# Attention's product with v in plain 32-bit floats, each head in its own half of TensorE's columns

## The chip, the cores and the metric

One core of one Trainium2 chip runs the whole kernel. The metric is the device time of one execution in microseconds (us), and lower is better. The engines are TensorE (PE, with its weight loads as PEld), VectorE (DVE), ScalarE (ACT), GpSimd (POOL) and SyncE (SP, which here only issues transfers).

## The reference

Attention with a threshold feeds a layer of 8 experts with two of them per token, and that feeds a dense layer. Only attention is touched:

```python
scores = q @ k.T / 8                          # 4 batches, 8 heads, 576 positions, 64 features
thresh = scores.max(-1) - tau
attn   = exp(where(scores >= thresh, scores, -1e9) - scores.max(-1))
out    = (attn / (attn.sum(-1) + 1e-9)) @ v
# x = out, heads side by side: (2304, 512)
# experts: gate and noise logits of x, top 2 of 8, relu(x @ w1) @ w2
# dense: elu(x @ w_in) @ w_out
```

## The kernel before

*Work units.* The 32 heads are handled as 16 pairs P, with s = 0 and 1 for the two heads of a pair. The 576 positions are four blocks of 128 (NB = 4) and a tail of 64. A pair has nine units u: unit 0 holds the tail rows of both heads, units 1 to 8 are one block of rows of one head (`ORDER`). Each unit goes through the same steps, which single letters name in the order lists:

- S `scores` (line 236): products of q and k into a double bank of PSUM
- R `rowmax` (261) on DVE, H `thresh` (263) on DVE (its ScalarE branch is never taken, since `HA` is always false), E `expo` (270) on ACT
- M `mask` (275) on DVE: exponentials below the threshold become 0, and their sum is taken. For unit 0 POOL then copies the last 64 columns once more (line 294)
- T `trans` (302): four transposes on PE, so that keys lie on partitions
- A, L, C `evac_trans` (328): PSUM to SBUF, as two tiles of rounded floats (`F32R`), high (`pth`) and low (`ptl`). High is a copy on ACT (line 324 or 320). Low is what is left of the sum: for seven units a PE product with the negative identity `negi` subtracts the high half in PSUM, and ACT copies the rest (325, 326); for units 0 and 2 DVE subtracts (321).

Per pair come the steps t, a, d `tails` (345): transposes of the tail keys, and their high and low halves; p, q `pv` (366): the product with v, for each head and each of two chunks of query columns (320 and 256 wide); W `weigh`: one over the sums; f, g `fin` (395): products that turn the result back to rows and multiply it with the gate weights `wx`, a copy on ACT, and the scaling on POOL.

*The product with v.* v is split by POOL into high and low halves (`split_v`, 226), side by side in 128 columns. One `pv` call makes ten products (four blocks and the tail, each with the high and the low half of the exponentials) into all 128 partitions: 64 of v's high half and 64 of its low half. The two are added in `fin`, whose weights hold the identity twice. `fin`'s operands (`ot`, `wx`) are plain 32-bit floats.

*Order.* PE, ACT and DVE run in an order written by hand: the strings `FIRST` (pair 0 alone), `CYCLE` (each further pair; the number behind the dot says how many pairs back the step belongs to) and `REST` (what is left). G and F advance the expert gate of a finished batch, W and X other small steps. POOL and SP are ordered by the program and its dependences. `load(P + 2)` fetches q, k and v two pairs ahead; `split_q` and `split_k` on POOL and copies on SP's queue prepare the next pair's scores.

After attention come the experts (from line 759) and the dense layer (from line 1029), which the change leaves as they are.

Of the kernel before, what the change touches and what calls it, by code (L numbers as in the profile page):

```python
# [25 lines left out]
def fused_kernel(ctx, tc, q, k, v, tau, w_gate, noise, wm, wf, out):  # L26
# [56 lines left out]
    negi = consts.tile([128, 128], F32R, name="negi")  # L83
    dve.tensor_scalar(negi, iot, 0.0, -1.0, op0=OP.is_equal, op1=OP.mult)
# [29 lines left out]
    for nm, sh, dt, n in (("qr", [128, S], F32, 2), ("kr", [128, S], F32, 2), ("vr", [128, NU, D], F32, 2),  # L114
# [31 lines left out]
    wx = apool.tile([128, HP, D + 4 * E], F32, name="wx", bufs=1)  # L146
# [4 lines left out]
    def load(P):  # L151

        t = []
        for nm, src in (("qr", q), ("kr", k), ("vr", v))[0 if P else 2:]:
            x = apool.tile([128, S], F32, name=nm)
# [4 lines left out]
        RAW[P] = t  # L160

# [64 lines left out]
    def split_v(P):  # L226
        vr = RAW[P][-1].rearrange("p (i d) -> p i d", d=D)
        vs = apool.tile([128, 2 * NB, 2, D], F32R, name="vs")
        vt = vts[P % 2]
        for hi, lo, x in [(vs[:, :, 0], vs[:, :, 1], vr[:, :2 * NB])] + \  # L230
                [(vt[r, s, 0], vt[r, s, 1], vr[r, 2 * NB]) for s, r in ((0, slice(0, 64)), (1, slice(64, 128)))]:
            rounded(hi, x, pool)
            pool.tensor_tensor(lo, x, f32(hi), op=OP.subtract)
        VS[P] = (vs, vt)

# [39 lines left out]
    def mask(g):  # L275
# [38 lines left out]
    def halves(P, s, c):  # L314
        if (P, s, c) not in PTH:
            PTH[P, s, c] = tuple(apool.tile([128, NB, CW[c]], F32R, name=f"pt{x}{s}{c}", bufs=1) for x in "hl")
        return PTH[P, s, c]

    def evac(o_hi, o_lo, ps):
        return (lambda: act.activation(o_hi, ps, AF.Copy),  # L320
                lambda: dve.tensor_tensor(o_lo, ps, f32(o_hi), op=OP.subtract))  # L321

    def evac_pe(o_hi, o_lo, ps):
        return (lambda: act.activation(o_hi, ps, AF.Copy),  # L324
                lambda: pe.matmul(ps, negi, o_hi, start=False, stop=True, skip_group_check=True),  # L325
                lambda: act.activation(o_lo, ps, AF.Copy))  # L326

    def evac_trans(g):

        P, u = divmod(g, NU)  # L330
        ps = PS_.pop(g)
        if u:
            i, s = ORDER[u]
            h, l = halves(P, s, i // 2)
            c = (i % 2) * 128 + (TAIL if s and i < 2 else 0)
            r = (evac_pe if VP(P, u) and P not in EVEN else evac)(h[:, :, c:c + 128], l[:, :, c:c + 128], ps)
            return [r[:1], r[1:-1], r[-1:]]
        r = []
        for s in range(2):
            h, l = halves(P, s, 0)  # L340
            c = 0 if s else 256
            r.append(evac(h[:, :, c:c + 64], l[:, :, c:c + 64], ps[:, :, s * 64:s * 64 + 64]))
        return [x[0] for x in r], [], [x[1] for x in r]

    def tails(P, half):
        ps = mi(512)
        for n in range(2):
            turn(ps[:, n * 128:n * 128 + 128], P_[P, 2 * half + n][1][:, MAIN:MAIN + 128], F32R)
        if not half:
            turn(ps[:, 256:384], PTB[1][:, MAIN:], F32R)  # L350
        cols = ((0, 0, 256),) if half else ((64, 0, 320), (0, 320, 64))

        def high():
            PTT[P, half] = tuple(apool.tile([128, 384 - 128 * half], F32R, name=f"ptt{x}{half}", bufs=1) for x in "hl")
            for o, i, n in cols:
                act.activation(PTT[P, half][0][:, o:o + n], ps[:, i:i + n], AF.Copy)

        def low():
            for o, i, n in cols:
                h, l = (x[:, o:o + n] for x in PTT[P, half])  # L360
                dve.tensor_tensor(l, ps[:, i:i + n], f32(h), op=OP.subtract)
        return high, low

    OC = ((256, 0), (S, S + 320))

    def pv(P, s, ch):
        vs, vt = VS[P]
# [3 lines left out]
        ps = mi(512)
        steps = [(kb, x) for kb in range(NB + 1) for x in range(2)]
        for m, (kb, x) in enumerate(steps):
            if kb < NB:
                lhs = vs[:, s * NB + kb]
                rhs = PTH[P, s, ch][x][:, kb]
            else:
                lhs = vt[:, s]
                o = 0 if s or ch else TAIL
                rhs = PTT[P, ch][x][:, o:o + n]  # L380
# [899 lines left out]
```

## Time and profile before

| what | value |
|---|---|
| median of 3 runs | 1244.54 us (1244.17 to 1246.15) |
| the profiled execution itself | 1239.1 us |
| its span, first to last instruction | 1237.3 us |
| mean granted TensorE clock | 0.985 |

The profile is one execution of its own. Rows of a trace give the start and the duration of an instruction; TensorE's instructions overlap, so the distance between two starts tells what one costs the engine, and the duration tells how long it is in flight. A plain 32-bit product appears as two records, each with a weight load.

### The profile page before, as it was taken

The numbers are of one execution on the slowest core, as the hardware profiler recorded it, in microseconds if no ns is written. First come the engines' busy times: TensorE is split into PE (matmuls) and PEld (weight loads), VectorE is DVE, ScalarE is ACT, GpSimd is POOL, SyncE is SP. The second block draws the span as 40 slices with busy tenths as digits, with TensorE's granted clock in tenths as the row PEclk, the third lists the DMA queues.
The fourth block names the chain that finished last, engine by engine and source line by source line (L and its number), as shares of the span: only waits on it lengthen the run. The fifth ranks groups of instructions, "written<-read, shape, count | busy, mean of one in ns | idle before, by whom it ended". The sixth has DMA issues, their size and how long they took to land.

```text
span 1237.3 us, 20812 instructions
## 1 busy us (share of the span) xinstructions
PE 1187.9 (96%) x7675; PEld 1088.4 (88%) x7675; DVE 751.7 (61%) x1663; ACT 650.7 (53%) x1324; POOL 320.5 (26%) x502
## 2 busy tenths in 40 slices
PE   4999999989889999999999999899999999999997
PEld 3899999989779998998998898788999889999996
DVE  6899999979764886656665557355343333333332
ACT  3899999879633443333333332256554554444443
POOL 8546657786650111000010001311011010000000
PEclk8999999999989999999999999899999999999999
DMA  7577674552466785465555544443123021010000
GB/s 214 170 209 205 191 213 124 157 174 80 171 235 241 233 269 180 163 194 166 185 178 154 177 138 171 153 165 126 43 63 92 17 70 41 11 51 19 1 17 20
DMA packets 64044, 169.50 MB, mean 137 GB/s; under 512 B 9408, under 2 KB 9536, under 8 KB 58304
## 3 DMA queue, kind: packets, MB, share of 16 engines
q1 hardware_dynamic: 52768, 138.45, 36.2%
q0 software_dynamic: 5760, 18.88, 4.5%
q10 hardware_dynamic: 5408, 10.78, 2.4%
q8 instruction: 62, 1.02, 0.4%
q14 instruction: 46, 0.38, 0.1%
HBM read 97.72 MB, written 43.52 MB: 114 GB/s over the span
## 4 chain that ended last, share of the span: by engine, by line
PE 73%; issue 10%; DVE 6%; DMA 6%; POOL 3%; ACT 2%; SPq 0%; POOLq 0%; ACTq 0%; DVEq 0%
PE y L877 17%; PE h L861 16%; PE o L1070 11%; PE h L1051 11%; PE bank L252 6%; PE bank L381 5%; PE bank L164 3%; PE bank L408 2%; PE bank L325 2%; DMA yg<-ys_d,yslot 2%; DMA w<-in_moe_dram 1%; PE h L164 1%; DVE P L289 1%; DVE nmax L261 1%; POOL yg L774 1%
## 5 line engine op out<-in xcount | busy, mean ns | idle before, releaser
L1059 DVE SCALAR_TENSOR_TENSOR g<-fr,h 128x256 f32<-128x256 f32 x144 | 60.3, 420 | 173.1 <-ACT fr L1058 172.8
L864 ACT ACTIVATE hh<-h 128x320 fp32r<-128x320 f32 (+2 forms) x128 | 55.5, 434 | 159.1 <-PE h L861 149.6
L845 POOL TENSOR_TENSOR c<-c,c 128x512 int32<-128x512 int32 x32 | 41.4, 1293 | 372.1 <-DVE c L844 372.1
L261 DVE TENSOR_REDUCE nmax<-bank 128x1 f32<-128x576 f32 x144 | 107.6, 753 | 19.4 <-PE bank L252 17.7
L1057 ACT ACTIVATE fr<-h 128x256 f32<-128x256 f32 x144 | 54.9, 382 | 118.1 <-PE h L1051 118.0
L273 ACT ACTIVATE e<-bank,nmax 128x576 f32<-128x576 f32 x144 | 106.6, 748 | 15.9 <-DVE nmax L261 14.0
L252 PE MATMUL bank<-kT,qT 128*128 128x288 f32 x320 | 98.5, 323 | 16.3 <-DVE kT L191 8.2
L774 POOL DMA_INDIRECT yg<-ys_d,yslot x36 | 39.0, 1083 | 269.8 <-PE h L164 170.2
L865 DVE SCALAR_TENSOR_TENSOR hl<-h,hh 128x320 fp32r<-128x320 f32 (+2 forms) x128 | 62.3, 487 | 67.5 <-ACT hh L864 67.0
L289 DVE SCALAR_TENSOR_TENSOR P<-bank,thr,e 128x576 f32<-128x576 f32 x128 | 100.0, 807 | 3.8 <-ACT e L273 1.9
L1061 DVE TENSOR_TENSOR gl<-g,gh 128x256 fp32r<-128x256 f32 x144 | 61.0, 425 | 67.5 <-ACT gh L1060 66.6
L252 PE MATMUL bank<-kT,qL 128*128 128x288 f32 x320 | 92.7, 305 | 0.8 <-DVE qL L199 0.8
L1060 ACT ACTIVATE gh<-g 128x256 fp32r<-128x256 f32 x144 | 59.8, 416 | 63.4 <-DVE g L1059 63.4
L252 PEld LDWEIGHTS bank<-kT,qT 128*128 128x128 f32 x320 | 62.6, 196 | 23.5 <-DVE P L289 10.7
L326 ACT ACTIVATE ptl<-bank 128x512 fp32r<-128x512 f32 x107 | 65.0, 607 | 17.0 <-PE bank L325 15.7
L381 PE MATMUL bank<-pth,vs 128*128 128x320 f32 (+1 forms) x256 | 73.3, 309 | 0.0
L381 PE MATMUL bank<-ptl,vs 128*128 128x320 f32 (+1 forms) x256 | 69.8, 295 | 0.0
L324 ACT ACTIVATE pth<-bank 128x512 fp32r<-128x512 f32 x107 | 62.9, 596 | 8.4 <-PE bank L164 7.4
L164 PE MATMUL bank<-ident,P_r 128*128 128x128 f32 x576 | 63.8, 243 | 2.3 <-DVE ptl L321 1.6
L252 PEld LDWEIGHTS bank<-kT,qL 128*128 128x128 f32 x320 | 63.1, 197 | 2.3 <-DVE qL L199 1.0
L164 PEld LDWEIGHTS bank<-ident,P_r 128*128 128x128 f32 x576 | 61.1, 142 | 3.5 <-DVE ptl L321 1.8
L1058 ACT ACTIVATE fr<-fr 128x256 f32<-128x256 f32 x144 | 59.9, 417 | 4.1
(373 smaller groups left out, 3929.3 us busy)
## 6 DMA issues: line engine op xcount, KB each, us to landing
w<-in_moe_dram SPq DMA_DIRECT2D x36, 1024.0 KB, 6.3
cr<-in_ffn_dram SPq DMA_DIRECT2D x32, 512.0 KB, 4.5
xs_d<-t ACTq DMA_DIRECT2D x8, 1280.0 KB, 5.4
ys_d<-y SPq DMA_DIRECT2D x40, 256.0 KB, 2.3
xr<-xs_d SPq DMA_DIRECT2D x38, 256.0 KB, 3.5
qT<-qh SPq DMA_DIRECT2D x60, 144.0 KB, 3.4
wf_d<-c SPq DMA_DIRECT2D x32, 256.0 KB, 4.5
w<-wf_d SPq DMA_DIRECT2D x8, 1024.0 KB, 6.2
```

The source lines that it names most:

```text
L164: pe.matmul(o.bitcast(dt), x.bitcast(dt), ident.bitcast(dt), is_transpose=True, **{"start": True, "stop": True, **kw})
L252: pe.matmul(ps[:, hv, :S // 2], x[:, qc:qc + 128], kx[:, kc:kc + S // 2], start=(m == 0), stop=(m == n - 1))
L261: dve.tensor_reduce(ST[g][0], view(g), axis=AX.XY, op=OP.max, negate=True)
L273: act.activation(e, view(g), AF.Exp, bias=ST[g][0])
L289: dve.scalar_tensor_tensor(o.rearrange("p (a c) -> p a c", a=2), view(g), ST[g][1], E_.pop(g), op0=OP.is_ge, op1=OP.mult, accum_out=SU[P][ ...
L324: return (lambda: act.activation(o_hi, ps, AF.Copy), lambda: pe.matmul(ps, negi, o_hi, start=False, stop=True, skip_group_check=True), lam ...
L326: lambda: act.activation(o_lo, ps, AF.Copy))
L381: pe.matmul(ps[:, :n], lhs.rearrange("p a d -> p (a d)"), rhs, start=(m == 0), stop=(m == len(steps) - 1))
L861: pe.matmul(ps[:, :step], w[:, c, f * 128:(f + 1) * 128], x[:, c, o:o + step], start=(m == 0), stop=(m == 3 * NC1 - 1))
L877: pe.matmul(Y[t], h[:, t * 128:(t + 1) * 128], w[:, f], start=(first and m == 0), stop=(last and m == 2))
L1051: pe.matmul(ps, w[:, c, f * 128:(f + 1) * 128], x[:, c], start=(m == 0), stop=(m == 3 * NC1 - 1))
L1070: pe.matmul(O[i], h[:, i * 128:(i + 1) * 128], w[:, f], start=(un == f == m == 0), stop=(un == NU2 - 1 and f == UF - 1 and m == 2))
```

## The change

The exponentials and v are no longer split. `evac_trans` copies each transposed unit once, by ACT, into a plain 32-bit tile; `negi`, the low halves and `split_v` are gone. `pv(P, ch, part)` handles both heads of a chunk: head s writes partitions 64 s to 64 s + 63 of one bank, with 64 columns of v as weights, and products of the two heads alternate. The ten products of a chunk are issued in two parts, a (four) and b (six). The tail rows of v sit in four zeroed tiles `vt`, filled by two more loads per pair; v itself gets four buffers. The tail keys of both heads share one tile, with one more transpose, and the zeros behind unit 0 are set once in place of POOL's copy. One ACT copy empties both heads of a chunk. `fin` takes 128 query columns of both heads at once (160 output columns), and the tails in two halves. The three order lists are rewritten, with `SECOND` for the second pair.

```diff
-    negi = consts.tile([128, 128], F32R, name="negi")
-    dve.tensor_scalar(negi, iot, 0.0, -1.0, op0=OP.is_equal, op1=OP.mult)
...
-    wx = apool.tile([128, HP, D + 4 * E], F32, name="wx", bufs=1)
+    wx = apool.tile([128, HP, 2, D + 2 * E], F32, name="wx", bufs=1)
...
+        vt = vts[P % 4]
+        VS[P] = t[-1].rearrange("p (i d) -> p i d", d=D), vt
+        for s in range(2):
+            r = slice(s * 64, s * 64 + 64)
+            st = sp.dma_start(vt[r, s], v[P][r, 2 * NB * D:])
...
-    def split_v(P):
...
-        if HA(*divmod(g, NU)):
-            act.activation(thr, nmax, AF.Identity, scale=-1.0, bias=tneg)
-        else:
-            dve.tensor_scalar(thr, nmax, -1.0, tneg, op0=OP.mult, op1=OP.add)
+        dve.tensor_scalar(thr, nmax, -1.0, tneg, op0=OP.mult, op1=OP.add)
...
-        if u == 0:
-            pool.tensor_scalar(PTB[0][:, S:], PTB[0][:, MAIN:S], 1.0, 1.0, op0=OP.mult, op1=OP.mult)
...
+            act.activation(turned_p(P, s, i // 2)[:, :, c:c + 128], ps, AF.Copy)
+        else:
+            for s in range(2):
+                act.activation(turned_p(P, s, 0)[:, :, 256:], ps[:, :, s * 64:s * 64 + 64], AF.Copy)
...
-            turn(ps[:, 256:384], PTB[1][:, MAIN:], F32R)
+            for n, c in enumerate((MAIN, MAIN - 64)):
+                turn(ps[:, 256 + n * 128:384 + n * 128], PTB[1][:, c:c + 128], F32R)
...
+        if part == "a":
+            PV_[P, ch] = mi(512)
+        ps = PV_[P, ch][:, :n]
+        for kb in (range(2) if part == "a" else range(2, NB + 1)):
+            for s in range(2):
+                if kb < NB:
+                    lhs, rhs = vr[:, s * NB + kb], PTH[P, s, ch][:, kb]
+                else:
+                    lhs, rhs = vt[:, s], PTT[P, ch]
+                pe.matmul(ps[s * 64:s * 64 + 64], lhs, rhs, start=(kb == 0), stop=(kb == NB))
+        o = OC[ch]
+        return lambda: act.activation(OT[P][:, o:o + n], ps, AF.Copy)
...
+        for i in range(2):
+            c = OC[half] + i * 128
+            pe.matmul(ps[:, 2 * i * NX:2 * (i + 1) * NX], OT[P][:, c:c + 128],
+                      wx[:, j].rearrange("p a b -> p (a b)"), start=True, stop=True)
+        if not half:
+            for s in range(2):
+                pe.matmul(ps[s * 64:s * 64 + 64, n:n + NX], OT[P][:, MAIN:S], wx[:, j, s], start=True, stop=True)
...
+    pool.memset(PTB[0][:, S:], 0.0)
+    dve.memset(wx, 0.0)
...
+    CYCLE = """
+        E7.1 E8.1 H8.1 a0.1 M7.1 G.0 S1.0 M8.1 W.1 T6.1 G.0 R1.0 S2.0 R2.0 H1.0 G.0 H2.0 g1.2 E1.0 E2.0 T5.1 G.0 p0b.1
+        M1.0 A6.1 S4.0 G.0 M2.0 R4.0 A5.1 q0.1 G.0 E4.0 F.0 S3.0 R3.0 t1.1 E3.0 G.0 H4.0 H3.0 a1.1 T7.1 G.0 T8.1 A7.1
+        A8.1 f0.1 G.0 M4.0 S5.0 M3.0 R5.0 H5.0 G.0 T1.0 E5.0 T3.0 g0.1 G.0 M5.0 S0.0 R0.0 p1a.1 G.0 A3.0 F.0 A1.0 S6.0
+        T2.0 R6.0 G.0 E0.0 T4.0 p1b.1 H0.0 G.0 H6.0 E6.0 A4.0 M0.0 G.0 S7.0 q1.1 M6.0 A2.0 T0.0 G.0 S8.0 A0.0 t0.0 f1.1
+        G.0 p0a.0 R7.0 R8.0 H7.0 G.0
+    """.split()
```

## Rows read from the trace of the kernel before

**Rows 1.** The page's table of engines: busy us, share of the span, instructions.
```profile
PE 1187.9 (96%) x7675; PEld 1088.4 (88%) x7675; DVE 751.7 (61%) x1663; ACT 650.7 (53%) x1324; POOL 320.5 (26%) x502
```

**Rows 2.** Windows: from:to, length, then busy us (instructions) by engine, granted clock, DMA.
```profile
100.00:200.00 100.00, 100.00 (x809) 97.71 (x808) 95.68 (x244) 95.37 (x195) 59.62 (x116) 1.00 0.70 198
95.24:185.76 90.52, 90.52 (x732) 88.66 (x731) 86.72 (x221) 86.44 (x176) 55.09 (x107) 1.00 0.72 206
1000.00:1100.00 100.00, 99.90 (x647) 90.61 (x646) 34.74 (x79) 48.36 (x117) 5.02 (x5) 1.00 0.14 46
```

**Rows 3.** Timeline of TensorE at the end of attention: start, us, line, tiles, count.
```profile
330.98 3.12 PE L861 MATMUL h<-xb 128*128 128x256 f32 x24
```

**Rows 4.** Timeline of TensorE, the scores of one unit and the next work.
```profile
302.02 0.29 PE L252 MATMUL bank<-kT,qT 128*128 128x288 f32 x1
302.15 0.29 PE L252 MATMUL bank<-kT,qL 128*128 128x288 f32 x1
...
302.55 0.46 PE L164 MATMUL bank<-ident,P_r 128*128 128x128 f32 x4
```

**Rows 5.** Timeline of TensorE, products with v and with the negative identity.
```profile
304.82 0.32 PE L381 MATMUL bank<-ptl,vs 128*128 128x320 f32 x1
...
306.15 0.39 PE L325 MATMUL bank<-pth,negi 128*128 128x512 f32 x1
306.38 0.29 PE L252 MATMUL bank<-kT,qT 128*128 128x288 f32 x1
...
311.73 0.28 PE L381 MATMUL bank<-pth,vs 128*128 128x256 f32 x1
...
312.92 0.46 PE L164 MATMUL bank<-ident,P_r 128*128 128x128 f32 x4
```

**Rows 6.** Groups of instructions in five pairs (95.24 to 185.76): busy us, mean ns.
```profile
L326 ACT ACTIVATE ptl<-bank 128x512 fp32r<-128x512 f32 x35 | 21.3, 608 | 2.8 <-PE bank L325 2.4
L325 PE MATMUL bank<-pth,negi 128*128 128x512 f32 x35 | 14.7, 419 | 0.0
L384 ACT ACTIVATE ot<-bank 128x320 f32<-128x320 f32 (+1 forms) x20 | 8.2, 410 | 0.0
L321 DVE TENSOR_TENSOR ptl<-bank,pth 128x256 fp32r<-128x256 f32 (+1 forms) x15 | 7.2, 507 | 0.4
L233 POOL TENSOR_TENSOR vs<-vr,vs 128x512 fp32r<-128x512 f32 x5 | 6.4, 1278 | 0.0
L361 DVE TENSOR_TENSOR pttl<-bank,ptth 128x256 fp32r<-128x256 f32 (+2 forms) x15 | 5.2, 371 | 0.0
```

**Rows 7.** Timeline of TensorE, six transposes and the products behind them.
```profile
130.59 0.62 PE L164 MATMUL bank<-ident,P_r 128*128 128x128 f32 x6
131.05 0.38 PE L381 MATMUL bank<-pth,vs 128*128 128x320 f32 x1
131.27 0.31 PE L381 MATMUL bank<-ptl,vs 128*128 128x320 f32 x1
```

**Rows 8.** Timeline of TensorE, the gate products of one pair and what follows.
```profile
181.25 1.98 PE L408 MATMUL bank<-wx,ot 128*128 128x80 f32 x16
183.06 0.40 PE L410 MATMUL bank<-wx,ot 128*128 128x96 f32 x2
183.24 0.48 PE L325 MATMUL bank<-pth,negi 128*128 128x512 f32 x1
183.56 0.29 PE L252 MATMUL bank<-kT,qT 128*128 128x288 f32 x1
```

**Rows 9.** The chain of waits: the gate products once a pair (start, us).
```profile
127.01 1.81 PE bank L408 x16
...
199.81 1.81 PE bank L408 x16
...
281.45 1.81 PE bank L408 x16
```

**Rows 10.** TensorE's waits (whole run; 205 to 331 us), and one SP issue.
```profile
PE bank L164 <- POOL PT L294: 7.6, 3, 3.4
PE bank L164 <- POOL PT L294: 4.3, 2, 3.2
221.27 0.33 SPq L156 DMA_DIRECT2D qr<-in_q_dram  x1
```

More of the change, by code (lines that the diff above doesn't have):

```diff
@@ L154, in load @@
         for nm, src in (("qr", q), ("kr", k), ("vr", v))[0 if P else 2:]:
-            x = apool.tile([128, S], F32, name=nm)
+            x = apool.tile([128, S], F32, name=nm, bufs=4 if nm == "vr" else 2)
             st = sp.dma_start(x, src[P])
@@ L312, in trans, with turned_p @@
             turn(ps[:, kb], src[:, c + kb * 128:c + kb * 128 + 128], F32R, start=(kb == 0), stop=(kb == NB - 1))
-    def halves(P, s, c):
+    def turned_p(P, s, c):
         if (P, s, c) not in PTH:
-            PTH[P, s, c] = tuple(apool.tile([128, NB, CW[c]], F32R, name=f"pt{x}{s}{c}", bufs=1) for x in "hl")
+            PTH[P, s, c] = apool.tile([128, NB, CW[c]], F32, name=f"pt{s}{c}", bufs=2)
         return PTH[P, s, c]
[L319 to L326, printed above, removed]
     def evac_trans(g):
@@ L333, in evac_trans @@
             i, s = ORDER[u]
[L334 to L343, printed above, removed]
+            c = (i % 2) * 128
+            act.activation(turned_p(P, s, i // 2)[:, :, c:c + 128], ps, AF.Copy)
+        else:
+            for s in range(2):
+                act.activation(turned_p(P, s, 0)[:, :, 256:], ps[:, :, s * 64:s * 64 + 64], AF.Copy)
     def tails(P, half):
@@ L349, in tails @@
         if not half:
-            turn(ps[:, 256:384], PTB[1][:, MAIN:], F32R)
[L351 to L367, printed above, removed]
+            for n, c in enumerate((MAIN, MAIN - 64)):
+                turn(ps[:, 256 + n * 128:384 + n * 128], PTB[1][:, c:c + 128], F32R)
+        def out():
+            t = PTT[P, half] = apool.tile([128, CW[half]], F32, name=f"ptt{half}", bufs=1)
+            act.activation(t[:, :256], ps[:, :256], AF.Copy)
+            if not half:
+                for n in range(2):
+                    r = slice(n * 64, n * 64 + 64)
+                    act.activation(t[r, 256:], ps[r, 256 + n * 192:320 + n * 192], AF.Copy)
@@ L368, in pv @@
+        return out
+    OC = (256, 0)
+    def pv(P, ch, part):
+        vr, vt = VS[P]
         if P not in OT:
-            OT[P] = apool.tile([128, 2 * S], F32, name="ot")
+            OT[P] = apool.tile([128, S], F32, name="ot")
         n = CW[ch]
[L371 to L380, printed above, removed]
-            pe.matmul(ps[:, :n], lhs.rearrange("p a d -> p (a d)"), rhs,
-                      start=(m == 0), stop=(m == len(steps) - 1))
@@ L393, in weigh, with fin @@
         dve.reciprocal(rinv, rinv)
-    def fin(P, s):
+    def fin(P, half):
         b, j = divmod(P, HP)
-        h = 2 * j + s
         rinv = SU[P][1]
-        if h == 0:
+        if P % HP == half == 0:
             XB[b] = xpool.tile([128, NB, H, D], F32, name="xb", bufs=3)
@@ L587, in fused_kernel @@
         qLs.append(t)
-        t = apool.tile([128, 2, 2, D], F32R, name=f"vt{i}", bufs=1)
-        pool.memset(f32(t), 0.0)
+    for i in range(4):
+        t = apool.tile([128, 2, D], F32, name=f"vt{i}", bufs=1)
+        pool.memset(t, 0.0)
         vts.append(t)
+    pool.memset(PTB[0][:, S:], 0.0)
+    dve.memset(wx, 0.0)
     first = first_qk()
@@ L635, in run @@
             weigh(P)
[L636 to L654 removed]
+        elif x == "t":
+            AFTER[what, P] = tails(P, int(g))
+        elif x == "p":
+            AFTER["p" + g[0], P] = pv(P, int(g[0]), g[1])
+        elif x == "f":
+            AFTER[what, P] = fin(P, int(g))
+        elif x == "a":
+            AFTER["t" + g, P]()
+        elif x == "q":
+            AFTER["p" + g, P]()
+        elif x == "g":
+            for f in AFTER["f" + g, P]:
+                f()
+        else:
+            {"S": scores, "R": rowmax, "H": thresh, "E": expo, "M": mask, "T": trans,
+             "A": evac_trans}[x](P * NU + int(g))
     def gate_step(at):
@@ L673, in beside @@
                 f(P + 1)
-        if u == 1 and 0 < P < NP:
-            split_v(P)
         x = P // HP - 1
@@ L732, in fused_kernel @@
             u = 0
-            if c == NP:
-                EVEN.add(NP - 1)
-            for x in REST if c == NP else CYCLE if c else FIRST:
+            for x in REST if c == NP else SECOND + CYCLE if c == 1 else CYCLE if c else FIRST:
                 what, lag = x.split(".")
@@ L742, in fused_kernel @@
                 elif 0 <= P < NP:
+                    if (what, P) in done:
+                        continue
+                    done.add((what, P))
                     run(what, P)
```

103 lines of the change are left out of this document (34 added, 69 removed).

## The prediction

> **What bounds the kernel now.** I read the table of engines first [rows 1]: TensorE is busy 96% of the span, and its weight loads 88%, the other engines far less. An average over the span says little, so I read busy time by stretch next [rows 2]. Between 100 and 200 us, in attention, TensorE (100%), VectorE (96%) and ScalarE (95%) are all full; after attention (1000 to 1100) only TensorE is. The granted clock is 1.00 in these rows, the 2.4 GHz level. The change touches attention alone, which ends at 331 us, where the experts' first product starts [rows 3]. What follows is bound by TensorE and by loads issued behind attention's last steps, so I let it move as a block.
>
> "Busy" counts overlapping latencies, so I rebuilt one pair of heads from distances between starts. Scores: four products of 288 columns start at 302.02 and the next work at 302.55, 0.133 us each [rows 4]; 40 a pair, 5.3 us. Products with v: nine steps of 320 columns from 304.82 to 306.15, 0.148 each; ten of 256 columns from 311.73 to 312.92, 0.119 each [rows 5]. A pair has two blocks of ten of each: 5.3 us. The product with the negative identity (306.15 to 306.38) takes 0.23, and there are seven a pair [rows 5, 6]: 1.6 us. Transposes: six in 0.46 us, and the first product behind them takes 0.22 instead of 0.148 [rows 7], so about 0.09 each with that entry; 41 a pair, 3.7 us. The products with the gate weights (`fin`): sixteen records in 1.81 us, two in 0.18, and the next product is late by 0.09 (0.32 instead of 0.23) [rows 8]: 2.1 us. Sum 18.0 us. The period by the chain of waits is (199.81 - 127.01)/4 = 18.2 us [rows 9]. So TensorE is what a pair costs. Four later pairs, with the gate's work, take (281.45 - 199.81)/4 = 20.4 [rows 9]: 8.8 us more in all, 4.3 of them TensorE waiting for POOL's copy of the tail (line 294) [rows 10].
>
> **The change, part by part.** *Removed from TensorE:* 5.3 us of products with v and 1.6 us with the negative identity, per pair.
>
> *Added: the products in plain 32-bit floats*, 20 a pair, ten per chunk, each 64 output columns wide. The nearest row is `fin`, plain floats too: a product there is two records, each with its own weight load (8 products of 80 columns give 16 records), and a record of 80 columns takes 1.81/16 = 0.113 us [rows 8]. At the pace of 0.46 ns per column in rows 5, one sweep over 80 columns is 0.037, so 0.076 is something else. It may be a constant per record, with one sweep: a record of 320 columns would take 0.148 + 0.076 = 0.22, of 256 columns 0.19. It may be two sweeps and a constant of 0.039: 0.33 and 0.28. Or all of it is per column: 0.45 and 0.36. The 96-column records (0.18 + 0.09 for two, the change of kind included) are longer than the 80-column ones, which speaks against the first; I take two sweeps, with half of the constant covered by the other head: 0.315 and 0.255.
>
> Whether the two heads' records run side by side, no row shows: no product of the kernel before writes only half of the partitions. Side by side, with each record of one half beside one of the other, a pair costs ten record times per chunk: 10 x (0.315 + 0.255) = 5.7 us. One after the other it is 11.4. I take 5.7: outputs lie in separate partitions, weights in separate columns, and the two operands come from different tiles, so nothing in the program joins them.
>
> Here the Trainium skill speaks on both sides. "TensorEngine Tiling (Array Packing)", Key Properties, lets different tiles load weights and multiply in parallel, which would give 5.7. "TensorE: Matmul & The Clock Gate", Part 3, says that a weight load overlaps a running product only when the row group differs. Both heads use all 128 rows, so by that rule it would be nearer 11.4. No row here decides.
>
> *Other TensorE terms:* `fin` becomes eight records of 160 columns (two sweeps 0.147 and 0.039: 1.5 us) and four of 80 columns by halves (0.23 to 0.45, say 0.34): 1.8, so -0.3. One transpose more: +0.09. Four parts of the v product that are entered and left in another mode: 0.07 each as in rows 7, +0.3 (0 to 0.6). Sum per pair: -5.3 - 1.6 + 5.7 - 0.3 + 0.1 + 0.3 = -1.1, cautiously -1.0; over 16 pairs -16 us.
>
> *ScalarE and VectorE* lose, per pair, the low halves: 21.3/5 = 4.3 us on ScalarE and (7.2 + 5.2)/5 = 2.5 on VectorE [rows 6]. Half of the copies of `ot` go as well (8.2/10 = 0.8), since one copy now serves two heads. From 86.4/5 = 17.3 and 86.7/5 = 17.3 [rows 2] they fall to about 12.2 and 14.8. TensorE's 17.1 stays the longest; VectorE is the next bound, at 14.8. The threshold stays on VectorE as before, so that edit is worth nothing.
>
> *POOL* loses the split of v (6.4/5 = 1.3 us for the large subtraction alone [rows 6]) and the copy at line 294. TensorE waited 7.6 us for that copy, three times, once 3.4 us at the start [rows 10]. Now VectorE's own result releases the transpose. Next late are the scores of the next pair, whose operands come from POOL's splits, which are relieved too; I keep 5.5 of the 7.6. In the gate pairs 8.8 - 4.3 = 4.5 us are left of the excess, where VectorE's gate work lengthens the pair; it is relieved by 2.5 against TensorE's 1.0. I keep 2.
>
> *Loads:* two small loads a pair for the tail of v, on SP, at 0.33 us of issue or somewhat more [rows 10]. They go out two pairs ahead, so they cost nothing; without that cover the copies of q and k behind them on SP would be 1 us late. The memset of the gate weights' tile falls where VectorE waits for its first data.
>
> Sum: -16 - 5.5 - 2 = -23.5. The profiled execution took 1239.1 us (span 1237.3), so 1215.6 for one like it. The median of the runs is 5.4 above that, so 1221.
>
> **The rivals.** *A, the halves take turns* (the slower end). If a head's record, or its weight load, waits for the other head's, the v product costs 11.4: +5.7 x 16 = +91, so 1221 + 91 = 1312. It decides from a v product of about 5.7 + 23.5/16 = 7.2 us a pair: above that the kernel is slower. For it: no row shows two streams at once.
>
> *B, a change of half costs.* Each entry into another kind cost 0.07 in rows 7. If every one of the 20 products pays it, +1.4 a pair, +22: 1243, no change. The Trainium skill, "TensorE: Matmul & The Clock Gate", Part 3, has three column tiles at 2.38 times the speed; an estimate at the same efficiency for two, 1.59, gives 11.4/1.59 = 7.2 us and the same time.
>
> *C, one sweep per record:* 10 x (0.22 + 0.19) = 4.1, 1.6 less a pair, 25 us: 1196. VectorE's 14.8 would then be just below TensorE's 15.5. Against it: the longer 96-column records.
>
> *D, all of it is per column:* 10 x (0.45 + 0.36) = 8.1, +2.4 a pair, +38: 1259.
>
> **How the numbers follow.** Forecast 0.50 (1208 to 1234), A 0.18, B 0.14, C 0.12, D 0.06. Leaving out A and the very ends, the range is 1195 to 1260 (0.80). Within 0.2%, 2.5 us, is what a measurement can't tell from no change. Faster: the forecast, C and half of B less a little, 0.70; same 0.07; slower A, D and some rest, 0.23.
>
> **What would show it.** Right: two records, one of each head, that start within a few tens of nanoseconds; a chunk of 320 columns in about 3.2 us; a period near 17 us; no wait of TensorE for POOL's copy; VectorE idle 2 us a pair. Wrong: the records of the two heads evenly spaced, the chunk at 6 us, period 22 and more (A); 0.22 or 0.45 a record (C, D); or a period that stays at 18 with TensorE idle, where the order written by hand binds.

## The result and the profile after

The changed kernel takes 1208.2 us (median; 1207.8 to 1210.8), the kernel before 1245.0 us on the same chip (1244.2 to 1246.2). The ratio is 0.971, with an interval of 0.969 to 0.973: 36.8 us faster, where 23.5 were forecast. The profiled execution took 1208.1 us, with a span of 1206.3.

The page's table of engines after, as in [rows 1], and below it the first window of [rows 2] (from:to, length, busy us and instructions of TensorE, weight loads, VectorE, ScalarE and POOL, granted clock, DMA):

```profile
PE 1165.9 (97%) x7488; PEld 1012.3 (84%) x7488; DVE 717.5 (59%) x1560; ACT 591.4 (49%) x1201; POOL 275.6 (23%) x425
```

```profile
100.00:200.00 100.00, 97.65 (x766) 74.90 (x768) 87.17 (x219) 76.51 (x154) 53.24 (x106) 1.00 0.69 190
```

In attention TensorE is no longer full: 97.7 us of 100. VectorE fell from 95.7 to 87.2, ScalarE from 95.4 to 76.5. Attention ends, at the experts' first product, 23.4 us earlier than in [rows 3], by the timeline of TensorE:

```profile
307.58 0.39 PE L834 MATMUL h<-xb 128*128 128x256 f32 x1 [0.22 <-ACT xb L694]
```

The product with v is seen best in windows of a few hundredths of a microsecond, where the timeline of TensorE shows one group of records at a time (start, us, count):

```profile
150.77 0.49 PE L352 MATMUL bank<-pt,vr 128*64 128x320 f32 x2
151.09 0.44 PE L352 MATMUL bank<-pt,vr 128*64 128x320 f32 x2
151.36 0.44 PE L352 MATMUL bank<-pt,vr 128*64 128x320 f32 x2
```

Records come two by two (one of each head, as experiments 1 and 5 show), and the next two start 0.27 us later. The busy time of those windows shows the weight loads:

```profile
150.95:151.00 0.05, 0.05 (x2) 0.02 (x2) 0.05 (x2) 0.05 (x1) 0.00 (x0) 1.00 0.97 348
151.20:151.25 0.05, 0.05 (x4) 0.04 (x2) 0.05 (x1) 0.05 (x1) 0.00 (x0) 1.00 0.36 138
```

In each, two weight loads (second group) are in progress while two to four products run. The timeline of a whole pair, with what stands behind each part:

```profile
150.77 1.30 PE L352 MATMUL bank<-pt,vr 128*64 128x320 f32 x8
152.00 0.40 PE L247 MATMUL bank<-kT,qT 128*128 128x288 f32 x1
152.24 0.29 PE L247 MATMUL bank<-kT,qL 128*128 128x288 f32 x1
152.36 0.29 PE L247 MATMUL bank<-kT,qT 128*128 128x288 f32 x1
...
153.93 1.30 PE L352 MATMUL bank<-pt,vr 128*64 128x320 f32 x8
155.06 0.71 PE L352 MATMUL bank<-ptt,vt 128*64 128x320 f32 x4
155.70 0.40 PE L247 MATMUL bank<-kT,qT 128*128 128x288 f32 x1
...
161.78 1.08 PE L352 MATMUL bank<-pt,vr 128*64 128x256 f32 x8
162.80 0.40 PE L247 MATMUL bank<-kT,qT 128*128 128x288 f32 x1
...
164.17 1.08 PE L352 MATMUL bank<-pt,vr 128*64 128x256 f32 x8
165.09 0.60 PE L352 MATMUL bank<-ptt,vt 128*64 128x256 f32 x4
165.62 0.40 PE L247 MATMUL bank<-kT,qT 128*128 128x288 f32 x1
```

From start to the next work, the first chunk takes 1.23 + 1.77 = 3.00 us and the second 1.02 + 1.45 = 2.47: 5.47 us a pair. Behind each of the four parts the first product of scores takes 0.24 instead of 0.13 us.

The chain of waits, as in [rows 9], has the gate products once a pair:

```profile
98.14 0.61 PE bank L378 x4
...
184.98 0.62 PE bank L378 x4
```

That is (184.98 - 98.14)/5 = 17.37 us a pair. TensorE's waits (us, times, longest), as in [rows 10]:

```profile
PE bank L247 <- DVE P L281: 10.3, 21, 1.4
PE bank L247 <- DVE kT L196: 8.2, 1, 8.2
```

None is left for POOL's copy. What TensorE waits for now in attention is the mask (line 281), which frees a bank for the next scores: 0.2 us in a steady pair, the rest at the start, in the pairs with the gate's work and at the end.

**Where the 36.8 us came from.** A second profile of the kernel before (1244.7 us, nearer its median than the first, 1239.1) is compared with the one of after. Periods run from one pair's first row maximum to the next.

| stretch (us) | before, first profile | before, second | after | second to after |
|---|---|---|---|---|
| first pair | 21.6 | 21.7 | 21.4 | -0.3 |
| second pair | 19.8 | 21.0 | 17.8 | -3.2 |
| eight pairs behind it | 145.4 | 145.2 | 139.0 | -6.2 |
| last five periods (gate work) | 100.1 | 104.1 | 92.7 | -11.4 |
| second to last, together | 265.2 | 270.3 | 249.5 | -20.8 |
| last pair's first row maximum to experts' first product | 34.6 | 40.5 | 27.1 | -13.4 |
| experts | 484.1 | 478.9 | 478.0 | -0.9 |
| dense layers | 422.2 | 422.0 | 420.7 | -1.3 |

The two profiles of before differ among themselves by 4 to 6 us in the gate pairs, at the end and in the experts, so a row of either can't be taken for the kernel's. Nearly all of the gain is attention: 34.5 us against the second profile, of which 6 are the steady pairs and 25 the gate pairs and the end; 23.4 us against the first, of which 6.4 are the steady pairs, 7.4 the gate pairs and 7.4 the end. The order lists do not have the first row maximum of a pair at the same place: in the new ones, part a of the first pair's product and nine more transposes run ahead of the second pair's. So the first row and the end are best read together.

The whole of attention, from the first row maximum to the experts' first product, does not depend on such marks. By windows, the first profile of before, the second, and after:

```profile
9.59:330.98 321.39, 301.47 (x2353) 288.53 (x2352) 290.84 (x783) 276.67 (x562) 209.12 (x395) 0.97 0.60 173
```

```profile
9.54:342.02 332.48, 307.54 (x2353) 294.58 (x2352) 293.06 (x783) 276.65 (x562) 209.24 (x395) 0.96 0.57 168
```

```profile
9.52:307.58 298.06, 281.93 (x2166) 214.87 (x2165) 254.29 (x680) 217.57 (x440) 164.61 (x319) 0.99 0.66 187
```

TensorE is busy for 19.5 us less than in the first profile and 25.6 less than in the second, and idle for 3.8 and 8.8 less. A part of the busy time is its clock: before, the granted clock was 0.88 and 0.79 (first and second profile) in the second pair, 0.93 and 0.86 in the last gate pair but one, and 1.00 and 0.92 at the end; after, it is 1.00 from the second pair on. So most of the second pair's gain is the clock.

### The profile page after: what moved, and what is told of

It reads as the page before. It is cut to its first block, busy times and chain, and to the rows that moved or that the text cites. A ratio compares the mean times of both kernels' runs of the same rounds, so it can differ in the third digit from the quotient of the medians.

```text
span 1206.3 us, 20167 instructions
## 1 busy us (share of the span) xinstructions
PE 1165.9 (97%) x7488; PEld 1012.3 (84%) x7488; DVE 717.5 (59%) x1560; ACT 591.4 (49%) x1201; POOL 275.6 (23%) x425
## 4 chain that ended last, share of the span: by engine, by line
PE 87%; DVE 6%; DMA 3%; issue 2%; ACT 1%; POOL 1%; SPq 0%; ACTq 0%; DVEq 0%; POOLq 0%
PE h L834 17%; PE y L850 17%; PE h L1024 17%; PE o L1043 17%; PE bank L247 7%; PE bank L352 6%; PE bank L169 3%; DVE nmax L256 2%; PE h L169 1%; DMA wf_d<-c 1%; DVE P L281 1%; PE bank L378 1%; DMA w<-in_moe_dram 1%; DMA yg<-ys_d,yslot 1%; ACT e L265 0%
## 5 line engine op out<-in xcount | busy, mean ns | idle before, releaser
L247 PE MATMUL bank<-kT,qT 128*128 128x288 f32 x320 | 105.3, 345 | 20.4 <-DVE P L281 10.3
L352 PE MATMUL bank<-pt,vr 128*64 128x256 f32 (+1 forms) x512 | 76.4, 419 | 0.0
L312 ACT ACTIVATE pt<-bank 128x512 f32<-128x512 f32 x128 | 71.4, 599 | 4.2 <-PE bank L169 3.6
L169 PEld LDWEIGHTS bank<-ident,P_r 128*128 128x128 f32 x576 | 58.2, 142 | 9.1 <-issue 6.2
L352 PEld LDWEIGHTS bank<-pt,vr 128*64 128x64 f32 x512 | 31.8, 136 | 20.1 <-issue 3.6
L834 PE MATMUL h<-xh,w20h 128*128 128x320 f32 (+2 forms) x120 | 38.9, 324 | 0.0
```

The source lines that it names most:

```text
L169: pe.matmul(o.bitcast(dt), x.bitcast(dt), ident.bitcast(dt), is_transpose=True, **{"start": True, "stop": True, **kw})
L247: pe.matmul(ps[:, hv, :S // 2], x[:, qc:qc + 128], kx[:, kc:kc + S // 2], start=(m == 0), stop=(m == n - 1))
L312: act.activation(turned_p(P, s, i // 2)[:, :, c:c + 128], ps, AF.Copy)
L352: pe.matmul(ps[s * 64:s * 64 + 64], lhs, rhs, start=(kb == 0), stop=(kb == NB))
L834: pe.matmul(ps[:, :step], w[:, c, f * 128:(f + 1) * 128], x[:, c, o:o + step], start=(m == 0), stop=(m == 3 * NC1 - 1))
```

## The experiments

Each ratio is to the kernel before, on the same chip.

**1. The heads one behind the other.** The same twenty products a pair, in another order.

```diff
-        for kb in (range(2) if part == "a" else range(2, NB + 1)):
-            for s in range(2):
+        for s in range(2):
+            for kb in (range(2) if part == "a" else range(2, NB + 1)):
```

> The kernel after, with one change: in each part of the product with v all products of head 0 are issued, then all of head 1. Theory (the two records that start 0.007 us apart belong to the two heads, and TensorE starts records in order): records of one half must follow each other, so only the record at the seam has a partner; a part of 8 records of 320 columns takes about 7 x 0.27 = 1.9 us instead of 1.23, a pair about 9 instead of 5.5, and the kernel about 1208 + 16 x 3.5 = 1265 (1245 to 1285). Rival (the two records that start together are the two sweeps of one product, in whatever half): nothing changes, 1208 +- 3, and the pairs of starts stay.

Measured: 1227.6 us, ratio 0.987 (0.985 to 0.989); period 18.46. Neither the theory's 1265 nor the rival's 1208 came. In the first part (two products of each head) records still start in twos. In the second part (three each) they do so only in the middle; the timeline of TensorE there:

```profile
162.64 1.35 PE L352 MATMUL bank<-pt,vr 128*64 128x320 f32 x6
163.77 0.43 PE L352 MATMUL bank<-ptt,vt 128*64 128x320 f32 x1
163.83 0.43 PE L352 MATMUL bank<-pt,vr 128*64 128x320 f32 x1
164.04 0.43 PE L352 MATMUL bank<-ptt,vt 128*64 128x320 f32 x1
164.09 0.43 PE L352 MATMUL bank<-pt,vr 128*64 128x320 f32 x1
164.36 0.70 PE L352 MATMUL bank<-ptt,vt 128*64 128x320 f32 x2
165.00 0.40 PE L247 MATMUL bank<-kT,qT 128*128 128x288 f32 x1
```

The first head's tail (`ptt`, its last step) runs beside the second head's earlier steps (`pt`). The part takes 165.00 - 162.64 = 2.36 us instead of 1.77; two such parts a pair explain most of the 1.1 us of period. So TensorE starts records of the other half beside those of this half though they stand behind them in the program, but only about four records ahead: at the start and the end two records run alone.

**2. The kernel before without POOL's copy.** The copy at line 294 is replaced by zeros set once and one more transpose.

```diff
-        if u == 0:
-            pool.tensor_scalar(PTB[0][:, S:], PTB[0][:, MAIN:S], 1.0, 1.0, op0=OP.mult, op1=OP.mult)
...
```

> The kernel before, with one part of the change alone: POOL's copy of unit 0's tail is replaced by zeros set once and one more transpose per pair. Theory of the prediction (5.5 of the 7.6 us that TensorE waits for that copy come back, the transpose costs 16 x 0.09 = 1.4): 4 us faster, 1241 against 1245, and no wait for POOL in the trace. Rival (what TensorE waited for there is late anyway, another wait takes its place): within 1.5 us of before, and the waits for VectorE's mask or for the next pair's scores grow by what the copy's wait loses.

Measured: 1240.9 us against 1244.1, ratio 0.998 (0.997 to 0.999): 3.2 us, nearer the theory's 4 than the rival, though the interval of 1 to 4 us reaches into both. No wait for POOL's copy is left. In the profile (against the second one of before, experiment 3) the first pair is 2.6 us and the second, at a higher granted clock, 1.6 us shorter. The last five periods are 2 us longer in sum and the end (40.7) is as before. So what came back is the wait at the start. Late in attention, where [rows 10] have two waits for the copy (3.2 and 1.1 us), two others stand:

```profile
PE bank L407 <- ACT ptl L324: 3.2, 1, 3.2
PE bank L164 <- DVE ptl L319: 2.9, 1, 2.9
```

Both are for low halves of the exponentials, which the change removes. The second profile of before, in which the copy is still made, has two such waits as well (3.9 and 3.1 us) and no late wait for POOL, so the late ones of [rows 10] do not come in every execution.

**3. The kernel before once more,** unchanged, for a second profile.

> The kernel before, unchanged, for a second profile. The profiled execution of before was 5.9 us below the median of its runs, and the experts' stage behind attention took 6 us less in the kernel after than in it, with the same instructions. Theory (loads of the experts' weights run at a rate that differs from execution to execution, which decides only just behind attention): the distance from attention's end to the dense layer's first product differs from the first profile's 484.1 us by 2 us or more, while attention ends within 0.5 us of 331.0. Rival (the stage is the same in each execution of the same kernel, and the change shortened it): 484.1 +- 1.

Measured: 1244.7 us. The experts' stretch took 478.9 instead of 484.1 us, as the theory had it (476.3 to 479.8 in every other profile here), so the 6 us by which it seemed shorter after the change are no gain of the change. But attention ended at 342.0 and not at 331.0, which neither had expected. The end of attention by windows: the first profile of before, this one, and after:

```profile
296.40:331.00 34.60, 31.99 (x268) 30.80 (x266) 28.67 (x90) 26.38 (x57) 19.07 (x38) 1.00 0.33 112
```

```profile
301.50:342.00 40.50, 34.29 (x266) 32.86 (x265) 29.07 (x90) 26.44 (x57) 19.03 (x38) 0.92 0.28 103
```

```profile
280.50:307.60 27.10, 24.92 (x204) 18.57 (x203) 18.92 (x51) 18.27 (x38) 13.89 (x30) 1.00 0.39 135
```

At the same granted clock (first and third window) TensorE is busy for 7.1 us less and idle for 2.2 instead of 2.6. This profile's end is 5.9 us longer than the first's: 3.6 us of idle time, and 2.3 of busy time at a clock of 0.92. Its timeline of TensorE has the two longest waits, and behind them a stretch at a slower pace:

```profile
324.79 0.53 PE L164 MATMUL bank<-ident,P_r 128*128 128x128 f32 x4 [2.04 <-issue]
328.48 1.00 PE L164 MATMUL bank<-ident,P_r 128*128 128x128 f32 x6 [3.15 <-DVE ptl L321]
...
332.16 0.47 PE L381 MATMUL bank<-pth,vs 128*128 128x320 f32 x1
332.42 0.47 PE L381 MATMUL bank<-ptl,vs 128*128 128x320 f32 x1
```

These steps are 0.26 us apart, not 0.148 [rows 5]: the granted clock is 0.50 there (331 to 333 us), the lower level of 1.2 GHz, behind two waits of 2 and 3 us.

**4. The gate products half a pair later.** `f` and `g` are the steps of the gate products in the order written by hand; `REST` (not shown) takes up those that are left over.

```diff
-E7.1 E8.1 H8.1 a0.1 M7.1 G.0 S1.0 M8.1 W.1 T6.1 G.0 R1.0 S2.0 R2.0 H1.0 G.0 H2.0 g1.2 E1.0 E2.0 T5.1 G.0 p0b.1
-M1.0 A6.1 S4.0 G.0 M2.0 R4.0 A5.1 q0.1 G.0 E4.0 F.0 S3.0 R3.0 t1.1 E3.0 G.0 H4.0 H3.0 a1.1 T7.1 G.0 T8.1 A7.1
-A8.1 f0.1 G.0 M4.0 S5.0 M3.0 R5.0 H5.0 G.0 T1.0 E5.0 T3.0 g0.1 G.0 M5.0 S0.0 R0.0 p1a.1 G.0 A3.0 F.0 A1.0 S6.0
-T2.0 R6.0 G.0 E0.0 T4.0 p1b.1 H0.0 G.0 H6.0 E6.0 A4.0 M0.0 G.0 S7.0 q1.1 M6.0 A2.0 T0.0 G.0 S8.0 A0.0 t0.0 f1.1
+E7.1 E8.1 H8.1 a0.1 M7.1 G.0 S1.0 M8.1 W.1 T6.1 G.0 R1.0 S2.0 R2.0 H1.0 G.0 H2.0 E1.0 E2.0 T5.1 G.0 p0b.1
+M1.0 A6.1 S4.0 G.0 M2.0 R4.0 A5.1 q0.1 f0.2 G.0 E4.0 F.0 S3.0 R3.0 t1.1 g0.2 E3.0 G.0 H4.0 H3.0 a1.1 T7.1 G.0 T8.1 A7.1
+A8.1 f1.2 G.0 M4.0 S5.0 M3.0 R5.0 H5.0 G.0 T1.0 E5.0 T3.0 g1.2 G.0 M5.0 S0.0 R0.0 p1a.1 G.0 A3.0 F.0 A1.0 S6.0
+T2.0 R6.0 G.0 E0.0 T4.0 p1b.1 H0.0 G.0 H6.0 E6.0 A4.0 M0.0 G.0 S7.0 q1.1 M6.0 A2.0 T0.0 G.0 S8.0 A0.0 t0.0
...
```

> The kernel after, with the gate products of each pair (steps f and g) put about half a pair later in the order, so that those of the last pair but one stand in the closing list too. Theory (the time from the last pair's first row maximum to the end of attention, 34.6 us before and 27.1 after, is set by how much TensorE work the order leaves for the closing list): this closing time grows by the 1.8 us of TensorE that it now holds in addition, 1.5 to 2.5 us, the period stays 17.4, and the kernel is about 2 us slower, 1210. Rival (the closing time is a chain of the last pair's own steps, in which added TensorE work fits): within 0.5 us of the kernel after.

Measured: 1222.3 us, ratio 0.982 (0.980 to 0.984). Neither 1210 nor 1208 came. The end is 1.2 us longer, a little less than the theory's 1.5 to 2.5, but the steady period is 18.25 instead of 17.37: TensorE waits 18.8 us for the mask, 31 times, where it was 10.3 and 21. The same step costs 0.9 us a pair more at another place of the order.

**5. One half of the columns.** Eight of the ten products of a chunk go to the lower half; the second head's are added to the first head's sums there.

```diff
-                pe.matmul(ps[s * 64:s * 64 + 64], lhs, rhs, start=(kb == 0), stop=(kb == NB))
+                z = s if kb == 0 else 0
+                pe.matmul(ps[z * 64:z * 64 + 64], lhs, rhs, start=(kb == 0), stop=bool(z) or (kb == NB and s == 1))
```

> The kernel after, with eight of the ten products of each chunk writing the lower half of the columns: head 1 keeps the upper half for its first block only, its other products are added to head 0's (so the output is not attention's). Number, size and order of the products are the same. Theory (a record waits for the one before it in its own half, and the two halves run beside each other): a 320-column chunk takes 18 records in a row, 18 x 0.267 = 4.8 us instead of 2.7, a pair 3.9 us more of TensorE, the period goes from 17.4 to about 21, the kernel to 1208 + 16 x 3.6 = 1266 (1250 to 1280), slower than before. Rival (what made the v product cheap is the narrow weights, 64 columns instead of 128, whichever half they go to): the period stays within 0.5 us of 17.4 and the kernel under 1217.

Measured: 1265.0 us, ratio 1.017 (1.013 to 1.020); period 21.22. This is slower than the kernel before, so what decides is that the two halves run side by side. Timeline of TensorE:

```profile
153.10 1.94 PE L353 MATMUL bank<-pt,vr 128*64 128x256 f32 x8
154.88 1.03 PE L353 MATMUL bank<-ptt,vt 128*64 128x256 f32 x4
```

Eight records of 256 columns in one half take 154.88 - 153.10 = 1.78 us, 0.22 each; in the changed kernel the same eight, four in each half, take 165.09 - 164.17 = 0.92.

**6. Copies given back to ScalarE.** A second copy of seven turned blocks a pair, as many as the kernel before had low halves by ScalarE, into a tile that nothing reads.

```diff
             act.activation(turned_p(P, s, i // 2)[:, :, c:c + 128], ps, AF.Copy)
+            if u != 2:
+                act.activation(apool.tile([128, NB, 128], F32, name="again"), ps, AF.Copy)
```

> The kernel after, with seven of ScalarE's low copies given back: after each unit but 0 and 2 ScalarE copies the transposed bank a second time into a tile that nobody reads (7 x 0.48 us of ScalarE a pair). Theory (the steady period is TensorE's; the relief of ScalarE and VectorE is what shortened the pairs with the gate's work and the closing list): steady period 17.4 to 17.8, gate pairs and closing list 4 to 10 us longer in sum, kernel 1214 to 1224. Rival (only TensorE's terms count): within 3 us of 1208. Second rival (the banks of PSUM are held longer, and TensorE waits for them in every pair): steady period 18.3 or more, kernel above 1228.

Measured: 1219.3 us, ratio 0.981 (0.978 to 0.984): seven copies of 0.6 us a pair on ScalarE cost 11 us. The time is in the range. In the profile (1215.6 us, the shortest of its runs) the gate pairs are 3.0 us and the end 1.6 us longer, 4.6 in sum, at the low end of the theory's 4 to 10. The steady period is 17.88, just above its 17.8, and costs as much: 0.5 us in each of eight pairs. TensorE waits 6.7 us, 15 times, for the copy of `ot`, once a pair.

**7. The split of v given back to POOL,** its result unread.

```diff
...
+        if u == 1 and 0 < P < NP:
+            split_v(P)
```

> The kernel after, with the split of v on POOL given back (six operations, 3.0 us of POOL a pair, into tiles that nobody reads). Theory (POOL, whose splits of q and k feed the next pair's scores, is late only where the scatters of a finished batch are in its way): steady period 17.4 unchanged, the two or three pairs with scatters and the start 2 to 6 us longer in sum, kernel 1210 to 1214. Rival (POOL's relief is worth nothing): within 1 us of 1208. Other rival (POOL carries most of what the gate pairs and the closing list gave): 15 us or more, 1223 and up.

Measured: 1216.5 us, ratio 0.978 (0.976 to 0.981): 8 us, more than the theory's 2 to 6. The steady period stays at 17.34 and the end at 27.15. The last five periods are 4.3 us longer in sum (two of them by 2.5 each, one shorter by 0.9) and the one ahead of them 1.1; the experts' stretch is 1.8 us longer. POOL's relief counts where the gate's work is.

**8. Fewer key blocks.** The products with key blocks 1 and 3 go; TensorE has some 2 us a pair less.

```diff
             for s in range(2):
+                if kb in (1, 3):
+                    continue
```

> The kernel after without the products of key blocks 1 and 3 (six of ten products per chunk are left, so the output leaves out half of the keys). It asks what bounds a pair next. Theory (TensorE still sets the period: 16.4 us of work and about 0.65 us of waiting for VectorE's mask): TensorE has 2.1 us less, VectorE's 14.8 comes into reach, the period falls by 1.2 to 2.0 us to 15.4 to 16.2, the kernel to 1176 to 1190. Rival (the order by hand and the chain row maximum, exponential, mask set the period): the period stays above 16.8 and the waits of TensorE for the mask grow to 30 us or more.

Measured: 1202.1 us, ratio 0.966 (0.963 to 0.969). The period falls by 0.52 only, to 16.85, as the rival had it (above 16.8), though TensorE's waits for the mask grow to 20.4 us and not to its 30:

```profile
PE bank L247 <- DVE P L281: 20.4, 46, 1.5
```

This cut returned a quarter of what it saved: the chain of row maximum, exponential and mask, and the order around it, are the next bound.

**9. A mask that reads no bank.** Tried as a version that might beat both.

```diff
-        dve.tensor_scalar(thr, nmax, -1.0, tneg, op0=OP.mult, op1=OP.add)
-        dve.scalar_tensor_tensor(o.rearrange("p (a c) -> p a c", a=2), view(g),
-                                 ST[g][1], E_.pop(g),
...
+        e = E_.pop(g)
+        dve.scalar_tensor_tensor(o.rearrange("p (a c) -> p a c", a=2), e,
+                                 ecut, e,
```

> The mask compares each exponential with exp(-tau), worked out once, instead of the score with the row's maximum less tau: the same condition up to rounding. The threshold per unit leaves VectorE (nine of about 0.21 us a pair) and a bank of scores comes free at the end of the exponential instead of at the end of the mask, 0.8 us earlier. Theory (after the change the scores wait for the chain of row maximum, exponential and mask, TensorE's own work being about 16.4 us a pair): TensorE's waits for the mask (10.3 us, 21 times) go, the steady period falls from 17.37 to 16.7 to 17.0, the kernel to 1199 to 1204 us. Rival (TensorE's own work and the hand-written order are the whole period): 17.3 and 1206 to 1209 us.

Measured: 1236.8 us, ratio 0.994 (0.991 to 0.996): 28 us slower than the changed kernel, outside both expectations. TensorE's waits for the mask at the scores are gone as the theory had it, but the transposes wait 19.1 us for it instead. Groups of instructions (busy us, mean ns), first of this kernel, then of the changed one:

```profile
L283 DVE SCALAR_TENSOR_TENSOR P<-e,ecut 128x576 f32<-128x576 f32 x128 | 126.3, 1001 | 22.6 <-ACT e L266 18.0 <-ACT ftmp L406 1.1 <-issue 0.2
L214 POOL TENSOR_TENSOR ql<-qr,qh 128x576 fp32r<-128x576 f32 x15 | 24.7, 1648 | 0.8
```

```profile
L212 POOL TENSOR_TENSOR ql<-qr,qh 128x576 fp32r<-128x576 f32 x15 | 21.3, 1419 | 1.1 <-POOL qh L173 0.2
L281 DVE SCALAR_TENSOR_TENSOR P<-bank,thr,e 128x576 f32<-128x576 f32 x128 | 101.1, 815 | 13.1 <-ACT e L265 10.0
```

The same instruction takes 1001 ns instead of 815 in the mean once both its inputs lie in SBUF, and POOL's split of q gets longer too. The timeline shows where:

```profile
149.51 1.81 POOL L214 TENSOR_TENSOR ql<-qr,qh 128x576 fp32r<-128x576 f32 x1
149.97 1.98 DVE L283 SCALAR_TENSOR_TENSOR P<-e,ecut 128x576 f32<-128x576 f32 x1
161.42 0.82 DVE L283 SCALAR_TENSOR_TENSOR P<-e,ecut 128x576 f32<-128x576 f32 x1
```

Beside POOL's work the mask took 1.98 us, alone 0.82: the two engines get into each other's way. Over 128 masks that is 24 us, on the path from the scores to the transposes; the thresholds that VectorE no longer works out (0.21 us each) had stood where the mask waits for the exponential anyway (10.0 us in the changed kernel's row). But not all of the 28 us are waits for masks. From the second pair's first row maximum to the end of attention, by windows, this kernel and the changed one:

```profile
33.14:335.67 302.53, 276.58 (x2093) 209.21 (x2090) 244.14 (x508) 206.98 (x420) 180.86 (x303) 0.96 0.58 167
```

```profile
30.95:307.58 276.63, 266.31 (x2092) 201.97 (x2090) 237.57 (x642) 207.19 (x421) 151.97 (x304) 1.00 0.65 186
```

TensorE is idle for 15.6 us more, and busy for 10.3 us more with the same work at a granted clock of 0.96. Another 2.2 us are lost ahead of the second pair.

The Trainium skill, "GPSIMD Engine Reference", section "Specifications", says that POOL's SBUF interfaces are shared with VectorE and contended for by VectorE instructions with two SBUF inputs; these rows agree.

**10. The second chunk's product half a pair later,** as far behind the scores as the kernel before had its last blocks, and its gate products with it (`REST`, not shown, follows).

```diff
-E7.1 E8.1 H8.1 a0.1 M7.1 G.0 S1.0 M8.1 W.1 T6.1 G.0 R1.0 S2.0 R2.0 H1.0 G.0 H2.0 g1.2 E1.0 E2.0 T5.1 G.0 p0b.1
-M1.0 A6.1 S4.0 G.0 M2.0 R4.0 A5.1 q0.1 G.0 E4.0 F.0 S3.0 R3.0 t1.1 E3.0 G.0 H4.0 H3.0 a1.1 T7.1 G.0 T8.1 A7.1
-A8.1 f0.1 G.0 M4.0 S5.0 M3.0 R5.0 H5.0 G.0 T1.0 E5.0 T3.0 g0.1 G.0 M5.0 S0.0 R0.0 p1a.1 G.0 A3.0 F.0 A1.0 S6.0
-T2.0 R6.0 G.0 E0.0 T4.0 p1b.1 H0.0 G.0 H6.0 E6.0 A4.0 M0.0 G.0 S7.0 q1.1 M6.0 A2.0 T0.0 G.0 S8.0 A0.0 t0.0 f1.1
+E7.1 E8.1 H8.1 a0.1 M7.1 G.0 S1.0 M8.1 W.1 T6.1 G.0 R1.0 S2.0 R2.0 H1.0 G.0 H2.0 E1.0 E2.0 T5.1 G.0 p0b.1
+M1.0 A6.1 S4.0 G.0 M2.0 R4.0 A5.1 q0.1 p1a.2 G.0 E4.0 F.0 S3.0 R3.0 p1b.2 t1.1 E3.0 G.0 H4.0 H3.0 q1.2 a1.1 T7.1 G.0 f1.2 T8.1 A7.1
+A8.1 g1.2 f0.1 G.0 M4.0 S5.0 M3.0 R5.0 H5.0 G.0 T1.0 E5.0 T3.0 g0.1 G.0 M5.0 S0.0 R0.0 G.0 A3.0 F.0 A1.0 S6.0
+T2.0 R6.0 G.0 E0.0 T4.0 H0.0 G.0 H6.0 E6.0 A4.0 M0.0 G.0 S7.0 M6.0 A2.0 T0.0 G.0 S8.0 A0.0 t0.0
...
```

> The changed kernel with the second chunk's product with v, and the products with the gate weights behind it, half a pair later, as far behind the scores as the kernel before had its last blocks. Theory (the end of attention is shorter because less work is left over behind the last scores): 2.5 us of product and 0.8 us of gate weights are added to what is left over, so from the last pair's first row maximum to the experts' first product it takes 30 to 32 us instead of 27.1; the steady period rises by 0.3 to 1.0 since the order is disturbed, and the kernel takes 1216 to 1226 us. Rival (it is shorter only because each product is cheaper and VectorE has less to do): 27 to 28 us there, and 1211 to 1222 us in all.

Measured: 1252.4 us, ratio 1.006 (1.003 to 1.008). The end takes 30.7 us: the theory's 30 to 32, not 27 to 28. The steady period was missed by far: 20 to 22 us, with TensorE waiting 41 us for masks, by the waits:

```profile
PE bank L247 <- DVE P L281: 20.8, 28, 1.7
PE bank L247 <- DVE PT L281: 20.2, 15, 2.2
```

From the second pair's first row maximum to the end of attention, by windows, as for the changed kernel in experiment 9:

```profile
31.64:352.49 320.85, 281.87 (x2096) 211.95 (x2092) 238.91 (x642) 207.29 (x421) 152.65 (x304) 0.96 0.56 161
```

TensorE is idle for 28.7 us more and busy for 15.6 us more. Steady pairs at a granted clock of 1.00 take 19.9 to 20.1 us, those in which it fell to 0.85 to 0.92 take 21.0 to 22.0. So the same instructions take 44 us more by their order: most of it in longer pairs at the full clock, the rest at the lower clock.

## Why the prediction was right, and where its sum was off

The direction and the mechanism were right, and the time lies in the range; the sum was 13 us short. By its steps:

- *The product with v, 5.7 us a pair, and entering and leaving, 0.3.* Together 5.9 of the 6.0: 5.47 from start to next work, and 0.11 behind each of the four parts. The sum of the two was right partly by luck, for both terms were mis-sized. Two heads' records start together, and the step is 0.27 us (0.22 at 256 columns): two sweeps, 2 x 320 columns at 2.4 GHz, worked out from the level that the granted clock of 1.00 stands for. The constant of 0.039 per record that I had read from the gate products is not there. In its place each part takes about 0.16 us more than its steps, and the scores behind it are 0.11 late.
- *The rivals.* *A* is refuted by experiment 5: one half alone costs twice as much. There a record of 256 columns alone in its half takes 0.22 us, as long as two side by side, so neither slows the other. *B*: no record pays for a change of half; the step between twos is the two sweeps. *C and D*: 0.27 is neither 0.22 nor 0.45.
- The Trainium skill, "TensorEngine Tiling (Array Packing)", Key Properties (tiles load and multiply in parallel), agrees with 0.92 against 1.78 us in experiment 5. The Trainium skill, "TensorE: Matmul & The Clock Gate", Part 3, has weight loads overlap running products only where row groups differ; here all rows are in use in both halves, and the windows of after show two loads in progress beside running products. The measurement decides. Already [rows 2] spoke against that rule, if not for the two halves: weight loads are busy for 97.7 of 100 us beside products that are busy for 100, in tiles of 128 rows.
- *The steady pair, -1.0.* Measured -0.8 over eight pairs. TensorE is busy for 17.14 us of the 17.38 (137.09 of 139.00 us between 48.72 and 187.72), where 17.1 was forecast, and waits 0.2 for masks. That the order written by hand binds was named as what would make the forecast wrong; experiments 4, 8 and 10 show that it does bind, by 0.9 us a pair when a step of 1.6 us is moved.
- *POOL's copy, -5.5.* Experiment 2 gained 3.2 us (1 to 4), less the transposes that it added, which were put at 1.4; so the copy may have been worth nearly as much as forecast. What failed is the place: the two late waits are not there in the second profile of before, only the one at the start is.
- *The gate pairs.* The last five periods have about -10 in the sum: -1.0 each, -2, and 3 for the copy's late waits. Measured -7.4 against the profile that the forecast was built on and -11.4 against the second. Experiments 6 and 7 have 3.0 for ScalarE's copies and 4.3 for POOL's split of v there; I had weighed VectorE's relief alone, which no experiment gives back.
- *The end of attention, -1.0 as for any pair.* This term is the furthest off: -7.4 by the first profile, -13.4 by the second. What was left over behind the last scores was five blocks of products with v, five units' transposes with their low halves, and the gate products of two pairs; now it is one chunk and a part, four units, and the gate products of one pair. TensorE has 7.1 us less there at the same clock. Some of it is moved and not saved: in the first pair, where TensorE had stood idle for 9 us, it is busy for 15.6 us instead of 12.2 (12.9 in the second profile). The other 6 us by the second profile are waits and the lower clock. Experiment 10 shows the size of such a part: a product of 2.5 us and its gate products put back cost 3.6 us.
- *The loads and the memsets, nothing.* The first pair, where they would show, went from 21.6 or 21.7 to 21.4, and with the copy away alone it had been 19.1 (experiment 2). But the new order has more of the first pair's work there, and TensorE is busy for 15.6 us and not 14.0, so the 2 us do not show a cost of the loads; that was not tried by itself.
- *The baseline.* In attention the forecast's -23.5 met the 23.4 us between the first profile and after, but by luck: it had too much in the first pair (-1.0 and 2.5 of the copy, against -0.2), the eight steady pairs (-8 against -6.4) and the gate pairs, and too little at the end. The 13 us lie in how the first profile was carried over. What follows attention was to move as a block, but that profile's experts took 4 to 8 us longer than any other's here: behind attention, after is 7.6 us shorter than it. And the 5.4 us from that profile to the median were kept, while the changed kernel has no such distance (1208.1 and 1208.2). The second profile shows what may stand behind the 5.4: late waits and a lower clock in attention, which after does not have.

## What to carry to other kernels

Two products with 64 output columns each, put in the two halves of the columns and issued in turn, run side by side at full pace: here a 32-bit product with two records is then nearly as cheap as the split one was (5.5 us a pair and 0.4 behind it, against 5.3), and all the work of making halves falls away from the other engines. Price the stretches at the ends and the irregular ones by themselves: what is left over behind the last step of a loop is a list with its own waits, and here it was worth as much as the steady loop or more. Take a second profile of the kernel before: the two here differ by 11 us in attention. With an order written by hand, a step moved by half a period can cost more than the step.

## What the runs showed of the hardware

- Records of the other half of the columns start beside earlier ones that still wait for their own half, about four records ahead (experiment 1). Within a half the rows show them in program order. Eight records of 256 columns took 0.92 us in two halves and 1.78 in one (experiment 5).
- VectorE's mask with two inputs in SBUF took 0.82 us alone and up to 2.1 beside POOL's work (experiment 9); with one of them in a bank, 0.79 to 0.82 in every pair of the changed kernel, beside POOL's work too.
- The same kernel's gate pairs and end of attention differ by 4 and 6 us between two executions (331.0 and 342.0 us at the end of attention). In the later one the granted clock was 0.92 at the end, behind two waits of 2 and 3 us.
- A step of products with v in the kernel before takes 0.148 us at a granted clock of 1.00 and 0.26 at 0.50 (experiment 3).
